# Four loads of v in one bunch, and an output projection one group later: a change to the order of work in a planned transformer kernel

## The chip, the cores and the metric

The kernel runs on one core of a Trainium2 chip. The metric is the device time of one execution in microseconds (us), from its start on the chip to its end; lower is better. The time of a version is the median of its runs.

The core has a matrix engine (TensorE, PE in the profile), a vector engine (VectorE, DVE), an engine for activations and copies (ScalarE, ACT), a general engine (GpSimd, POOL) and an engine that here does nothing but issue DMAs (SyncE, SP). Each works through its own list of instructions in order. ACT and POOL issue DMAs too, each from its own list. An instruction that waits for something holds up everything behind it on its engine.

## The reference

The input x has 2048 rows of 1024 bf16 numbers. The reference runs two kinds of layer, and the pair of them twice:

```python
x = A_x
x = x + _A_ref(_layernorm(x), A_wqkv, A_wo)
x = x + _B_ref(_layernorm(x), B_W_gate, B_W_up, B_W_down)
x = x + _A_ref(_layernorm(x), A_wqkv, A_wo)
x = x + _B_ref(_layernorm(x), B_W_gate, B_W_up, B_W_down)
```

`_A_ref` is attention over a dilated window. `x @ wqkv` (1024 x 3072) gives q, k and v with 32 heads of 32 numbers each. Row s looks at 8 rows only: s, s-2, ..., s-14 (rows before the first are masked). The 8 logits of a row and head are scaled, go through a softmax, weigh the same 8 rows of v, and the result is multiplied with `wo` (1024 x 1024).

`_B_ref` is a gated feed-forward layer: `gate = x @ W_gate` and `up = x @ W_up` (1024 x 3584 each), `h = relu(gate) * up`, and `h @ W_down` (3584 x 1024).

Both layers take the row-wise normalised x, (x - mean) / sqrt(var + eps), and add their result to x.

## The kernel before

**Tiling.** The rows are cut into 4 blocks of 512, and a block into 4 tiles of 128 rows. x stays in SBUF for the whole execution. All matrix products are groups of 8 (or 7) matmuls of 128 x 128 by 128 x 512 that add up in one PSUM accumulator; there are eight accumulators (`psum`, bufs=8). Weights come through a ring of five slabs (`ring`).

**Layers and blocks.** In the code layer 0 is the first attention, 1 the first feed-forward layer, 2 and 3 the second pair. TensorE first makes q, k and v of block 0 to block 3 of layer 0, one block after the other (`plan_proj`, L372). Then follow the feed-forward layer of block 0 (`plan_gu`, L728, then `plan_down`), and after it alternately pieces of attention and feed-forward work of the other blocks. The attention proper, between the projection and the multiplication with `wo`, has no matmul: DVE does it by products and additions.

**Block 0 of layer 0** has a way of its own to the logits, and the change lies there:

1. The matmuls of q and k give them feature-major. DVE multiplies and adds them over the features (`first_logits`, L473; `mul`, `add`) into two float32 buffers, `lacc0` and `lacc1`, with four of the eight window positions each.
2. Each half is stored to DRAM (`l_d<-lacc`, L528) and loaded back head-major (`lhm<-l_d`, L534), by two DMAs on SP. Both are planned in `turn(h)`, L525 to L542: the store 2.2 before the planned end of the half's last addition, the load 2.5 after it.
3. DVE folds the halves (`fold`), does the softmax (`soft_a`, `soft_b`; the exponential is ACT's), and then multiplies with v and adds, in 8 steps (`pv_mul` L629, `pv_add` L637 to L639). For this v must lie head-major in SBUF: `v_ready` (L664) plans four loads on SP, one for each tile of 128 rows (`vhm<-v_d`, L564). v itself was evicted by ACT from PSUM to `stage_v` and stored by a DMA that ACT issues.
4. The head outputs go to DRAM by a DMA of POOL (L640) and come back feature-major by four DMAs of SP (`load_o`, `oT<-o_d`, L648).
5. TensorE multiplies with `wo` (`plan_wo`, L701; matmuls L710, `acc_wo`), 2 groups for each of 4 tiles, and DVE adds each group to x (L717).

**Where step 5 stands.** TensorE does not wait idly for block 0's attention. It goes on with the projections of blocks 1 to 3. `wo_hook` (L819) names the group of block 3's projection behind which the eight groups of step 5 are put: `("q", 1, 1)`, the second of the four groups of the second half of q. `plan_proj` calls the hook behind that group (L466, L467), and the other groups of block 3 come after the eight.

**What follows.** With the addition of a tile of x, `plan_ln(1, 0)` (L212) begins the normalisation of block 0 for the feed-forward layer. For each tile: two sums on ACT (L238, L239). For each pair of tiles: four small DVE operations, the last giving `vpe` (L256 to L259), two small POOL operations `rstd` and `nb` (L260, L261), two normalisations on ACT (L267), and a transposing DMA on SP (`turn`, L273, `xnT<-xn_all`). The first gate group (L740, `acc_g`) of the feed-forward layer needs both transposes. The same function, with other times, normalises blocks 1 to 3 of layer 0 before their projections.

**What sets the order.** No scheduler reorders anything: the class `Plan` collects steps with planned times, and `run()` emits them sorted by time. TensorE's steps are laid end to end (`on_pe`, 0.216 for a matmul). DVE has a `chain`, the attention work, in its order, and `fixed` work with a due time (`on_dve`): before each link of the chain `_place_dve` first emits the fixed work that is due by then. The planned time at which a link ends sets the planned times of what hangs on it (`after`). DMAs have planned times only; their place among the other DMAs of the same engine comes from the sort. So a change to a planned time moves an instruction in the list of its engine. What it waits for at run time is then decided by the chip.

Completion of SP's and ACT's DMAs is counted on eight semaphores that are used in turn. In the programs' lists of waits each such DMA also waits for the one that used the same semaphore before it.

## Time and profile before

| | |
|---|---|
| time, median of 3 runs | 1617.26 us (1617.1 to 1617.5) |
| the profiled execution | 1618.13 us |
| its span, first to last instruction | 1616.4 us |
| granted TensorE clock, mean | 1.000 |
| share of the span in which the DMA engines work for SP's and ACT's queue (q1) | 66.9% |
| HBM read and written | 263.86 MB and 38.15 MB, 187 GB/s over the span |

In the profile a line such as `8.36 0.62 PE L404 MATMUL acc_v<-xnT,wqv 128*128 128x128 bf16 x8 [0.70 <-DMA wqv<-in_A_wqkv_dram]` reads: from 8.36 us after the start and for 0.62 us, TensorE ran 8 matmuls of line 404 that made `acc_v` out of `xnT` and `wqv`; before them it was idle for 0.70 us, and what ended the idle time was the landing of a DMA from `in_A_wqkv_dram` into `wqv`. SPq, ACTq and DVEq are the parts of an engine that issue DMAs or handle waits. A DMA has two times: the issue on the engine's queue, and the transfer up to its landing. Loads of a weight slab carry 1024 KB, a load of v 284 KB, a store of v 256 KB (section of DMA issues of the profile's page).

Where the first 200 us of the execution go, by TensorE's timeline: up to about 20 us the first pieces of v's projection for block 0, mixed with the transposes of the first tiles; then the rest of block 0's q, k and v up to 51.5 us; the projections of blocks 1 to 3, with the output projection of block 0 among the last, from 152.27 us; and from 190.26 us the feed-forward layer of block 0.

### The profile page before, as it was taken

Reading aid. Unit: us, or ns where it says so; the run is one execution under the profiler, and the core shown is the slowest. Engines: PE = TensorE matmul, PEld = TensorE weight load, DVE = VectorE, ACT = ScalarE, POOL = GpSimd, SP = SyncE. Lnnn points to the kernel's source line nnn. Section 1 sums busy time; section 2 is a strip of 40 time slices with the busy share of each in tenths; the row PEclk is TensorE's granted clock in tenths of the full one; section 3 lists DMA queues with packets and bytes.
Section 4 is the critical chain, followed back from the end, with each engine's and each line's share of the span. In section 5 each row is a group of like instructions: output and inputs, shape, how many; then the busy total and the mean of one; then the engine's idle time right before and its main releaser. Section 6 shows DMA issues by size and latency. Waiting matters only on the chain.

```text
span 1616.4 us, 19260 instructions
## 1 busy us (share of the span) xinstructions
PE 1610.0 (100%) x7656; PEld 745.6 (46%) x7656; DVE 1055.6 (65%) x1264; ACT 441.5 (27%) x703; POOL 126.2 (8%) x200
## 2 busy tenths in 40 slices
PE   9999999999999999999999999999999999999999
PEld 7444444444444444444444444444444444444444
DVE  6979999999999169860699517996998112211211
ACT  4642521305131241312413241133021311221110
POOL 2311000001011110011101110000000000000000
PEclk9999999999999999999999999999999999999999
DMA  8896797879966987669876699599856655574452
GB/s 256 227 242 154 203 215 201 209 177 214 220 182 204 243 187 210 197 212 232 194 204 195 209 226 219 165 274 225 224 163 194 178 169 163 176 188 151 157 167 68
DMA packets 444139, 319.02 MB, mean 197 GB/s; under 512 B 195696, under 2 KB 435728, under 8 KB 443792
## 3 DMA queue, kind: packets, MB, share of 16 engines
q1 hardware_dynamic: 414880, 285.59, 66.9%
q10 hardware_dynamic: 24368, 23.40, 4.8%
q0 software_dynamic: 4800, 8.80, 1.8%
q8 instruction: 60, 0.98, 0.3%
q14 instruction: 31, 0.25, 0.1%
HBM read 263.86 MB, written 38.15 MB: 187 GB/s over the span
## 4 chain that ended last, share of the span: by engine, by line
PE 93%; DVE 4%; DMA 2%; ACT 1%; issue 0%; SPq 0%; ACTq 0%; DVEq 0%
PE acc_u L740 24%; PE acc_g L740 24%; PE dacc L787 24%; PE acc_wo L710 7%; PE acc_v L404 5%; PE acc_k L404 5%; PE acc_q L404 4%; DVE pvt L629 1%; DVE lacc L522 1%; DVE pvt L637 1%; DMA l_d<-lacc 0%; DMA lhm<-l_d 0%; DVE prod L511 0%; DMA wqv<-in_A_wqkv_dram 0%; DVE pvt L638 0%; DMA oT<-o_d 0%
## 5 line engine op out<-in xcount | busy, mean ns | idle before, releaser
L740 PEld LDWEIGHTS <-ring 128*128 128x128 bf16 x3584 | 350.7, 98 | 422.9
L740 PE MATMUL acc_u<-xnT,ring 128*128 128x512 bf16 x1792 | 423.3, 379 | 0.0
L740 PE MATMUL acc_g<-xnT,ring 128*128 128x512 bf16 x1792 | 423.3, 379 | 0.0
L787 PE MATMUL dacc<-ring,hT 128*128 128x512 bf16 (+1 forms) x1820 | 388.1, 376 | 0.0
L755 DVE TENSOR_TENSOR hT<-acc_u,r 128x512 bf16<-128x512 f32 x224 | 154.2, 688 | 317.2 <-PE acc_u L740 312.1
L747 ACT ACTIVATE r<-acc_g 128x512 bf16<-128x512 f32 x224 | 133.5, 596 | 701.9 <-PE acc_g L740 690.4
L787 PEld LDWEIGHTS <-hT 128*128 128x128 bf16 x1820 | 178.1, 98 | 209.0
L404 PEld LDWEIGHTS <-ring 128*128 128x128 bf16 x1124 | 111.5, 100 | 124.0
L629 DVE TENSOR_TENSOR pvt<-a,vhm 128x4096 bf16<-128x4096 bf16 x64 | 146.2, 2284 | 0.1
L588 DVE TENSOR_TENSOR l<-l,pr 128x1024 f32<-128x1024 f32 x112 | 136.8, 1221 | 2.4
L578 DVE TENSOR_TENSOR pr<-qhm,khm 128x4096 bf16<-128x4096 bf16 x56 | 127.9, 2284 | 15.3 <-DMA khm<-k_d 15.3
L795 DVE TENSOR_TENSOR xb<-dacc,xb 128x512 bf16<-128x512 f32 (+1 forms) x49 | 32.8, 679 | 125.9 <-PE dacc L787 125.9
L404 PE MATMUL acc_k<-xnT,ring 128*128 128x512 bf16 x512 | 113.1, 379 | 0.0
L710 PE MATMUL acc_wo<-ring,oT 128*128 128x512 bf16 x512 | 111.8, 379 | 0.5 <-DMA oT<-o_d 0.5
L640 POOL DMA_DIRECT2D o_d<-ohm x64 | 35.2, 551 | 608.5 <-DVE ohm L639 594.6
L637 DVE TENSOR_TENSOR pvt<-pvt 128x2048 bf16<-128x2048 bf16 x64 | 78.1, 1221 | 1.3
L710 PEld LDWEIGHTS <-oT 128*128 128x128 bf16 x512 | 50.0, 98 | 61.2 <-DMA oT<-o_d 1.0
L404 PE MATMUL acc_v<-xnT,ring 128*128 128x512 bf16 (+1 forms) x356 | 76.1, 357 | 0.0
L260 POOL TENSOR_TENSOR rstd<-vpe,neg_half 128x2 f32<-128x2 f32 x30 | 32.0, 1066 | 552.5 <-DVE vpe L259 540.6
L414 ACT CAST stage_q<-acc_q 128x512 bf16<-128x512 f32 x56 | 32.2, 582 | 154.9 <-PE acc_q L404 150.6
L404 PEld LDWEIGHTS <-wqv 128*128 128x128 bf16 x556 | 52.0, 103 | 47.0 <-DMA wqv<-in_A_wqkv_dram 0.9
L588 DVE TENSOR_TENSOR l<-pr 128x1024 f32<-128x1024 bf16 x56 | 68.2, 1218 | 0.6
(88 smaller groups left out, 873.4 us busy)
## 6 DMA issues: line engine op xcount, KB each, us to landing
ring<-in_B_W_gate_dram SPq DMA_DIRECT2D x56, 1024.0 KB, 7.3
ring<-in_B_W_up_dram SPq DMA_DIRECT2D x56, 1024.0 KB, 5.6
ring<-in_B_W_down_dram SPq DMA_DIRECT2D x48, 1024.0 KB, 5.9
ring<-in_A_wqkv_dram SPq DMA_DIRECT2D x26, 1024.0 KB, 5.3
ring<-in_A_wo_dram SPq DMA_DIRECT2D x16, 1024.0 KB, 7.0
vhm<-v_d SPq DMA_DIRECT2D x32, 284.0 KB, 7.5
v_d<-stage_v ACTq DMA_DIRECT2D x32, 256.0 KB, 7.0
o_d<-ohm POOLq DMA_DIRECT2D x64, 128.0 KB, 3.7
```

Source lines behind the costliest of these rows:

```text
L404: nc.tensor.matmul(acc[:, t0 * P:t1 * P], lhsT=lhsT, rhs=xnT[(L, b)][:, t0:t1, kc, :], start=(kc == 0 and (nm, g, j) not in early), stop=( ...
L578: nc.vector.tensor_tensor(pr[:], st["q"][:], _ap(st["k"], HALO - DIL * w, [[HALO + P, DH], [1, P]]), op=ALU.mult)
L588: nc.vector.tensor_tensor(l[:], pr[:, 0:8] if i == 0 else l[:], pr[:, 8 * i + 8:8 * i + 16], op=ALU.add)
L629: nc.vector.tensor_tensor(tt[:], a_bc, v_sh, op=ALU.mult)
L637: nc.vector.tensor_tensor(tt[:, 0:4], tt[:, 0:4], tt[:, 4:8], op=ALU.add)
L640: nc.gpsimd.dma_start(_dram(o_d[b], g * DG * P, [[DH * P, P], [1, DG * P]]), o[:].rearrange("p d t -> p (d t)"))
L710: nc.tensor.matmul(acc[:], lhsT=st["oT"][:, c, t, :], rhs=ws[half]["t"][:, c, :], start=(c == 0), stop=(c == KC - 1))
L740: nc.tensor.matmul(acc[:], lhsT=w["t"][:, kc, (j % 4) * P:(j % 4 + 1) * P], rhs=xnT[(L, b)][:, :, kc, :], start=(kc == 0), stop=(kc == KC ...
L747: nc.scalar.activation(r[:], hold.pop(("g", j))[:], ACT.Relu)
L755: nc.vector.tensor_tensor(st["hT"][:, j, :], hold.pop(("u", j))[:], hold.pop(("r", j))[:], op=ALU.mult)
L787: nc.tensor.matmul(accs[(t, c0)][:], lhsT=st["hT"][:, j, t * P:(t + 1) * P], rhs=w["t"][:, jl, c0 - half * SLAB:c0 - half * SLAB + n], sta ...
L795: nc.vector.tensor_tensor(xt[:, c0:c0 + n], accs.pop((t, c0))[:], xt[:, c0:c0 + n], op=ALU.add)
```

## The change

Three edits, two of them in the plan of block 0's loads of v.

- In `v_ready` the four loads of v of block 0 had four planned times: the first two 0.8 apart, the last two just behind the planned time of the second load of logits (`tm["l_load"]`, which `turn(1)` wrote last). Now all four are planned 0.1 apart from the first's time on. The line that wrote `l_load` goes, since nothing reads it any more.
- In `wo_hook` the key `("q", 1, 1)` becomes `("q", 1, 2)`: the eight groups of block 0's output projection stand behind the third group of the second half of block 3's q.

In the lists of instructions this gives the following. On SP the third and fourth load of v stand directly behind the first two, ahead of the two transposes of block 2, the first store of logits and the first load of logits; before, they stood behind the second load of logits. On TensorE one group of `acc_q`, 8 matmuls, moves from behind the output projection to a place ahead of it. The planned times of what hangs on the projection move with it, so on DVE a product of a later block (L578) now stands ahead of the first additions of the output projection to x, and on ACT some evictions and issues of stores change places with the sums and normalisations of block 0. POOL's list is the same. No instruction is added or taken away.

```diff
@@ first_logits, turn(h)
                 plan.at(now - 2.2, store)
                 plan.at(now + 2.5, load)
                 tm[("l_in", h)] = now + 10.0
-                tm["l_load"] = now + 2.5
             return after
@@ plan_attn
         def v_ready():
             t = ends["v"] + 6.0
             if first:
-                return load((t, t + 0.8, tm["l_load"] + 0.1, tm["l_load"] + 0.2), (("v", v_d, ROW, HALO + P),))
+                return load(tuple(t + 0.1 * i for i in range(TPB)), (("v", v_d, ROW, HALO + P),))
@@ 
-    wo_hook = {("q", 1, 1): lambda: wo(0, 0)}
+    wo_hook = {("q", 1, 2): lambda: wo(0, 0)}
```

## The prediction

> **What bounds the kernel now.** I read the page first (totals, the chain that ended last), then the chain in order of time, then the timelines of PE, SP, DVE and ACT from 50 to 195 us, and the answers on single tiles for the time from a DMA's issue to its landing.

> ```profile
> span 1616.4 us, 19260 instructions
> ...
> PE 1610.0 (100%) x7656; PEld 745.6 (46%) x7656; DVE 1055.6 (65%) x1264; ACT 441.5 (27%) x703; POOL 126.2 (8%) x200
> ...
> PE 93%; DVE 4%; DMA 2%; ACT 1%; issue 0%; SPq 0%; ACTq 0%; DVEq 0%
> ```

> TensorE is busy for the whole span, at clock 1.00. A change elsewhere can therefore only add or remove a PE wait. The PE timeline has just one after the first 20 us, 0.47 us ahead of the first output projection:

> ```profile
> 152.27 13.99 PE L710 MATMUL acc_wo<-ring,oT 128*128 128x512 bf16 x64 [0.47 <-DMA oT<-o_d]
> ...
> 190.26 1.89 PE L740 MATMUL acc_g<-xnT,ring 128*128 128x512 bf16 x8
> ```

> The chain in order of time says what that wait stands on: block 0's attention, without a gap from the second half of its logits on.

> ```profile
> 80.22 2.30 DVE lacc L522
> 82.54 7.61 DMA l_d<-lacc
> 90.16 7.42 DMA lhm<-l_d
> 97.61 1.24 DVE lhm L549
> ...
> 145.07 2.29 DMA o_d<-ohm
> ...
> 147.63 4.59 DMA oT<-o_d
> ```

> Those two transfers sit in SP's queue behind what the change moves:

> ```profile
> 57.38 1.37 SPq L564 DMA_DIRECT2D vhm<-v_d  x2
> 65.14 6.08 SPq L273 DMA_TRANSPOSE xnT<-xn_all  x2
> 71.32 1.36 SPq L528 DMA_DIRECT2D l_d<-lacc  x1
> 78.67 0.34 SPq L534 DMA_DIRECT2D lhm<-l_d  x1
> 82.54 0.36 SPq L528 DMA_DIRECT2D l_d<-lacc  x1
> ```

> The second place with little slack is the first gate group at 190.26. It needs both transposes of the new normalised block 0; the second is issued at 181.81 and lands 6.2 us later, at 188.0. Its slack is 2.2 us.

> **The sum's base.** The profiled execution took 1618.13 us, 1.73 outside its span and 0.87 above the median of 1617.26. The sum is a difference in PE waits, and I add it to the median.

> **Part 1, the loads of v.** No work is added: four loads, all on SP, before and after. Two move from 90.5 to 58.8. Their issue (0.65 us each at 57.38) would lie in SP's pause from 58.75 to 65.14, where it waits for the normalisation of block 2. So much is free. But the program counts DMA landings on eight semaphores used in turn, and a DMA is issued only when the one before it on its semaphore has landed. With two more DMAs ahead, the lists of waits of the two programs give new partners:

> - The fourth load waits for a store of q that ACT issues at 61.85 and that lands 2.4 us later: 64.2.
> - Block 2's first transpose went at 65.14. It now waits for a store of k, issued at 65.62, landing after 3.4: 69.1, 3.9 later. The second follows 2.4 later at 71.5 and frees SP at 73.8. Both land by 79, and PE wants them at 92.9: covered by 14 us.
> - The first store of logits went at 71.32. It now waits for a store of q, issued 71.08, landing after 4.4: 75.5, so 4.2 late. It lands after 7.3, as before, at 82.8, and its load goes at 82.9.
> - The second store was ready when DVE ended at 82.52 and went at 82.54. SP now issues the first load just then, so it goes at 83.3: 0.8 late, with that load beside it.

> Its duration is the first unknown. Alone behind a nearly finished load it took 7.6. Weight loads of the same size that overlap took 10.4 and 10.9 (those issued at 184.0 and 186.7). The queues moved 317 GB/s from 82.5 to 90.2; load, store and two stores of v are 2.62 MB, 8.3 us at that rate, and about 1.5 us pass before a load's packets flow. I take 82.9 + 1.5 + 8.3 = 92.7, 2.5 late; the ends are 83.3 + 7.6 = 90.9 and 83.3 + 10.9 = 94.2. The second load took 7.4 with two loads of v behind it, the first one 6.1. I take its own 7.4, landing at 100.1, 2.5 late; the ends are 90.9 + 6.1 = 97.0 (0.6 early) and 94.2 + 7.4 = 101.6 (4.0 late).

> DVE waits for nothing but one exponential between 97.6 and 144.8, so all of this reaches the head outputs. ACT's exponential stands behind evictions that were themselves made later, 0.1 more. The shift is **2.6 us** (ends: 0.5 early, 4.1 late).

> The first load landing 4.2 us later also delays block 3's statistics on DVE and its normalisation on ACT, which holds up evictions: the one at 91.91 goes at 96.1. PE has eight accumulators of 1.73 us each, 13.8 us, so no wait. If that cover went, PE would stop near 101.

> **Part 2, the projection one group later.** One q group, 8 matmuls, 1.73 us, now runs before it. PE arrives at 152.27 - 0.47 + 1.73 = 153.5. The oT load lands at 152.2 + 2.6 = 154.8, and PE waits 1.3 where it waited 0.47: **+0.8**. With the loads as they were, this part alone would have removed the 0.47.

> **What is late next.** The same list of DVE instructions is planned anew. The adds of the projection's first tile stood before a product (L578, 2.28 us, 2.2 from start to start) and now stand after it. From 159.68 the add moves by 2.6 + 2.2. Row by row to the first pair's variance I get 0.3 more (one fold stands ahead of it now): 5.1 late. On ACT a DMA issue and an eviction of k now stand between the first pair's normalisation and the last tile's sums, and an eviction of v between the last two normalisations: 0.5, less 0.4 of waiting that goes, plus 0.7. So the second transpose is 5.9 late: 181.8 + 5.9 + 6.2 = 193.9. PE, 0.8 late, arrives at 191.1 and waits **2.8**.

> **Sum:** 0.8 + 2.8 = 3.6, with roundings 3.7 us: 1617.3 + 3.7 = **1621.0 us**. Nothing later is tight: the next groups waited for nothing before, and the weight loads behind the late transpose (184.0, 186.7) are wanted from 204.

> In that chain POOL's two small operations for the second pair are taken as before, 2.4 us. They took 1.59 and 0.69 there, 0.71 and 0.19 elsewhere; in both long cases they end right after the DVE operation beside them. Now short DVE operations stand beside them and then the 2.28 us product. Slipping in ahead of it saves 1.2; falling behind it costs 0.5.
> [...]

> **The rivals.**
> 1. *Not slower.* The two overlapping transfers take their low ends and POOL slips in. Then the shift is 0.5 early, PE finds oT landed, the second transpose is 2.8 - 1.2 = 1.6 late at 189.6, and PE comes at 189.8: 0.47 saved, 1616.8. It decides where the transpose is less than 1.8 late. For it: the 6.1 row, and two loads of v gone from 90.5. Against: DVE's new order alone costs 2.2.
> 2. *PE loses its clock in the wait.* The granted clock is 1.00 in every window, and no PE wait in this trace exceeds 1.5 us, so nothing here excludes that it falls in a longer one. If the first two groups after the wait ran at half speed, 2 x 1.73 us more: 1624.5. It decides if a wait of 2.8 us is long enough for that, of which the trace says nothing.
> [...]
> 3. *A small loss.* The semaphore partners land early, the shift is near 0.5, and the gate group waits about 1.5: net 1 us, 1618.3.
> 4. *The change gains.* PE can win back no more than 0.47 here, so faster by 0.2% is nearly excluded.

> **How the numbers follow.** What a measurement of this kernel can tell from no change is about 0.2%, 3.2 us: 1614.0 to 1620.5. The forecast case has 0.62 (its own range 1618.8 to 1622.8, about two thirds of it above 1620.5), the clock rival 0.13, the small loss 0.15, not slower 0.10. Slower: 0.41 + 0.13 = 0.54; within: 0.44; faster: 0.02. The range reaches from between the two small cases (1616.8 and 1618.3) to just past the clock rival, and leaves out the not-slower case and the tails: 1617.6 to 1624.6, about 0.83.

> **What would show it.** Right: first transpose of block 2 at about 69, logits stores at 75.5 and 83.3, second load landing near 100, PE waiting about 1.3 at L710 and 2.8 at L740. Wrong: if the two overlapped transfers land within 8 us, or the POOL pair takes under 1.3 us, the loss shrinks below 0.2%; if a clock under 1.00 follows PE's wait at L740, it is larger.

## The result, and the profile after

The changed kernel takes 1622.8 us (median of 8 runs, 1620.3 to 1624.1) against 1617.43 us of the kernel before, measured beside it: a ratio of 1.0028, with a 95% interval of 1.0017 to 1.0039. The forecast was 1621.0 us in a range of 1617.6 to 1624.6.

Its executions fall into two groups. Over all runs of the changed kernel in this study, nine took 1619.4 to 1621.5 us (median 1620.4) with a granted clock of 1.000, and ten took 1622.4 to 1624.1 us (median 1622.8) with 0.999 or 0.998. The profile is of the lower group: 1620.38 us beside a span of 1618.6. The page's totals:

```profile
span 1618.6 us, 19262 instructions
...
PE 1610.9 (100%) x7656; PEld 745.9 (46%) x7656; DVE 1055.8 (65%) x1264; ACT 441.4 (27%) x703; POOL 125.4 (8%) x200
```

The work is the same; the span is 2.2 us longer. TensorE's timeline shows where (start, busy time, and in brackets the idle time before and what ended it). Lines of the changed kernel's code from 541 on have numbers one lower than before:

```profile
154.05 13.99 PE L709 MATMUL acc_wo<-ring,oT 128*128 128x512 bf16 x64 [0.28 <-DMA oT<-o_d]
...
192.49 1.89 PE L739 MATMUL acc_g<-xnT,ring 128*128 128x512 bf16 x8 [2.01 <-DMA xnT<-xn_all]
```

The wait at the output projection went from 0.47 to 0.28 us, and a new one of 2.01 us stands at the first gate group. 0.24 us more had been lost before 121 us.

SP's timeline shows what became of the loads of logits:

```profile
57.18 9.14 SPq L563 DMA_DIRECT2D vhm<-v_d  x4
68.65 6.89 SPq L273 DMA_TRANSPOSE xnT<-xn_all  x2
76.14 0.69 SPq L528 DMA_DIRECT2D l_d<-lacc  x1
82.93 0.34 SPq L534 DMA_DIRECT2D lhm<-l_d  x1
83.36 0.39 SPq L528 DMA_DIRECT2D l_d<-lacc  x1
93.71 0.33 SPq L534 DMA_DIRECT2D lhm<-l_d  x1
```

The four loads of v occupy SP's queue for 9.14 us where two took 1.37, since the fourth goes only at 65.78, when a store of q on its semaphore has landed (65.77). Block 2's transposes go 3.5 us late, the first store of logits 4.8, its load 4.3, and the second load 3.6. The first transpose goes at 68.65, behind a store of k that landed at 68.57. The chain in order of time says what the first store of logits waited for last; it is a DMA with which it shares no data, a store of q that ACT had issued:

```profile
71.23 4.85 DMA q_d<-stage_q
...
76.14 6.77 DMA l_d<-lacc
```

This wait is not the whole delay. The two transposes themselves keep SP's queue until 75.54 (68.65 and 6.89 us), and the store of q adds 0.5 us to that.

The late first load also reaches the softmax. The statistics of block 3 stand behind it on DVE, and block 3's normalisations (L267) stand ahead of the exponential (L610) on ACT:

```profile
99.75 1.24 ACT L267 ACTIVATE xn_all<-xb,nb,rstd 128x1024 bf16<-128x1024 bf16 x1 [0.75 <-POOL nb L261]
...
101.90 1.24 ACT L267 ACTIVATE xn_all<-xb,nb,rstd 128x1024 bf16<-128x1024 bf16 x1 [0.45 <-ACT stage_v L414]
...
104.54 1.06 ACT L610 ACTIVATE L<-L 128x1024 f32<-128x1024 f32 x1 [0.44 <-ACT stage_q L414]
```

On POOL's timeline the second pair of small operations, which took 1.59 and 0.69 us before, has become short:

```profile
181.32 1.06 POOL L260 TENSOR_TENSOR rstd<-vpe,neg_half 128x2 f32<-128x2 f32 x1 [6.92 <-DVE vpe L259]
182.47 0.21 POOL L261 TENSOR_TENSOR nb<-neg,rstd 128x2 f32<-128x2 f32 x1
```

### The profile page after: what moved, and what is told of

Same layout as the page of the kernel before. It is cut to its first block, busy times and chain, and to the rows that moved or that the text cites. A ratio compares the mean times of both kernels' runs of the same rounds, so it can differ in the third digit from the quotient of the medians.

```text
span 1618.6 us, 19262 instructions
## 1 busy us (share of the span) xinstructions
PE 1610.9 (100%) x7656; PEld 745.9 (46%) x7656; DVE 1055.8 (65%) x1264; ACT 441.4 (27%) x703; POOL 125.4 (8%) x200
## 4 chain that ended last, share of the span: by engine, by line
PE 91%; DVE 4%; DMA 2%; issue 1%; ACT 1%; POOL 0%; ACTq 0%; SPq 0%; DVEq 0%; POOLq 0%
PE acc_g L739 24%; PE acc_u L739 24%; PE dacc L786 24%; PE acc_wo L709 6%; PE acc_q L404 5%; PE acc_k L404 5%; PE acc_v L404 4%; DVE pvt L628 1%; DMA xnT<-xn_all 1%; DVE l L587 1%; DVE pvt L636 1%; DMA l_d<-lacc 0%; DVE pr L577 0%; DMA lhm<-l_d 0%; DMA wqv<-in_A_wqkv_dram 0%
```

## The experiments

The theory after this result: the moved loads shift the semaphore partners and make the head outputs 1.5 to 2 us late; the later projection hides that at the output projection, but DVE's new order makes the second transpose of block 0 late, and TensorE waits at the first gate group; a wait of about 2 us costs TensorE its clock in some executions. Each part has a rival below. The medians, by the place of the loads of v and by the projection:

| loads of v \ projection | where it was | one group later | one group later, additions as before |
|---|---|---|---|
| as before | 1617.4 to 1617.7 (kernel before) | 1617.99 | 1617.17 |
| all four ahead of block 2's transposes | 1622.57 | 1622.8 and 1622.36 (changed kernel) | 1618.16 |
| two behind the first store of logits | 1617.45 | | 1617.62 |

### The loads of v alone

```diff
 (changed kernel)
-    wo_hook = {("q", 1, 2): lambda: wo(0, 0)}
+    wo_hook = {("q", 1, 1): lambda: wo(0, 0)}
```

> The changed kernel with the projection back behind the second group of q, so only the loads of v are moved. Theory (the gate group's wait comes mainly from the new place of the additions on DVE; the loads of v cost about 1.6 us on the way to the head outputs): TensorE arrives at the output projection near 152.0 us, oT lands as in the changed kernel near 154.0, so TensorE waits about 2.0 us there and none at the first gate group (second transpose landing near 190.4, TensorE there near 192.0). Time about 1.5 us above the kernel before, 1618.9. Rival (the late loads of logits alone carry the loss): the gate group still waits 2 us behind the other wait, time 1621 or more. Second rival (any wait of about 2 us can cost TensorE its clock): some executions 2 to 3 us above 1618.9, with a granted clock of 0.998 or 0.999.

Measured: 1622.57 us (1621.6 to 1623.8, 6 runs), ratio 1.0031 (1.0020 to 1.0043), and a clock of 0.998 or 0.999 in all six. So this part alone loses as much as the whole change (1622.36 us in the same set of runs), 3.7 us more than the theory's 1618.9. TensorE's timeline has all of the wait at the output projection and none at the gate group:

```profile
155.21 0.61 PE L709 MATMUL acc_wo<-ring,oT 128*128 128x512 bf16 x1 [3.39 <-DMA oT<-o_d]
156.03 15.93 PE L709 MATMUL acc_wo<-ring,oT 128*128 128x512 bf16 x61 [0.22 <-issue]
```

The stretches of the span around it (length, PE, PEld, DVE, ACT, POOL, granted clock, DMA share, GB/s) show the second rival at work:

```profile
154.00:156.00 2.00, 0.61 (x1) 0.28 (x3) 1.93 (x3) 0.00 (x0) 0.00 (x0) 0.51 1.18 303
...
160.00:161.00 1.00, 1.00 (x4) 0.33 (x3) 0.96 (x2) 0.00 (x0) 0.00 (x0) 0.57 1.44 156
161.00:162.00 1.00, 1.00 (x6) 0.49 (x5) 0.93 (x3) 0.00 (x0) 0.00 (x0) 1.00 1.46 154
```

From the end of the wait to about 160.9 the clock is 0.50, 5.7 us that do the work of 2.8. The wait was 1.4 us longer than expected: the last head outputs came 0.6 us later than in the profile of the changed kernel, and their store took 4.14 us, 0.6 more than there and 1.9 more than in the kernel before. Why the store takes so long is open; in the other profiles with the loads of v ahead it took 2.3 to 3.5 us.

### The projection alone

```diff
 (kernel before)
-    wo_hook = {("q", 1, 1): lambda: wo(0, 0)}
+    wo_hook = {("q", 1, 2): lambda: wo(0, 0)}
```

> The kernel before with only the projection moved behind the third group of q. Theory: oT lands at 152.2 us as in the kernel before, TensorE comes at 153.5 and waits for nothing there (0.47 us won); the additions stand behind a product of 2.28 us on DVE, so the second transpose of block 0 lands 2 to 3 us later, 190.1 to 191, and TensorE, there at 189.8, waits 0.3 to 1.2 us. Time within 0.7 us of the kernel before. Rival (the loads of v alone make the loss): no wait at all, 0.47 us faster. Clock 1.000 in every execution, since the wait is short.

Measured: 1617.99 us (11 runs), ratio 1.0003 (0.9994 to 1.0012), clock 1.000 throughout. As expected, 0.47 us are won at one place and nearly given back at the other:

```profile
190.15 1.89 PE L740 MATMUL acc_g<-xnT,ring 128*128 128x512 bf16 x8 [0.37 <-DMA xnT<-xn_all]
```

### The whole change, with the additions where they were

```diff
 (changed kernel, plan_wo)
-                plan.on_dve(e + T_EV, 0.7, add(half, t), ...)
+                plan.on_dve(e + T_EV - 8 * MM * ((L, b) == (0, 0)), 0.7, add(half, t), ...)
```

> The changed kernel, but the additions of block 0's output projection are given due times 1.73 us earlier, so that on DVE, ACT, SP and POOL they and all that hangs on them stand where they stood before; the loads of v and TensorE's order are those of the changed kernel. Theory: oT as in the changed kernel, a wait of about 0.3 us at the output projection; the second transpose lands 2.2 us or more sooner than in the changed kernel, near 190.2, TensorE comes at 190.2 to 190.5, and the gate group waits at most 0.3 us. Time 1617.3 (1617.0 to 1617.8), clock 1.000 in all executions. Rival (the late loads of logits carry the loss): a wait of 1.5 us or more stays, 1619 or more.

Measured: 1618.16 us (11 runs), ratio 1.0003 (0.9994 to 1.0012), 0.4 us above the range that was expected: most of the loss is gone (the changed kernel took 1622.36 us beside it), though the loads of v are still all ahead. Ten executions took 1617.9 to 1619.0 at clock 1.000, one 1621.83 at 0.999. It was this one that was profiled; there oT came late enough for a wait of 2.62 us at the output projection (and none at the gate group), and the clock fell behind it:

```profile
156.08 15.67 PE L709 MATMUL acc_wo<-ring,oT 128*128 128x512 bf16 x62 [2.62 <-DMA oT<-o_d]
```

```profile
156.00:157.00 1.00, 0.87 (x3) 0.41 (x5) 0.96 (x3) 0.00 (x0) 0.00 (x0) 0.76 1.33 254
157.00:158.00 1.00, 1.00 (x4) 0.39 (x3) 1.00 (x1) 0.00 (x0) 0.00 (x0) 0.50 1.39 218
...
160.00:161.00 1.00, 1.00 (x6) 0.43 (x5) 1.00 (x1) 0.00 (x0) 0.00 (x0) 1.00 1.45 148
```

So the order on DVE is what turns the late loads into the wait at the gate group. The expected wait of 0.3 us at the projection holds for most executions at best: in the profiled one the first store of logits went at 77.57 instead of 76.14 and the head outputs were stored 2.3 us later than in the profile of the changed kernel, with the same order on SP up to there.

### The changed kernel again

> The changed kernel, unchanged. Theory (its executions fall into two groups, 1620.3 to 1620.9 at clock 1.000 and 1622.7 to 1624.1 at 0.998 or 0.999, because TensorE loses its clock for one or two windows after the wait of about 2 us at the first gate group): the same two groups again, the gap between them 2 to 3 us; if the profiled execution is of the upper group, its granted clock falls below 1.00 only between 190 and 200 us. Rival (a cause elsewhere in the execution): the clock falls at another place, or the upper group is longer without it.

> The changed kernel again, for a profile of an execution of its upper group (ten of 17 so far). Theory: the wait at the first gate group is 2.0 to 3 us as in the two profiles of the lower group, and the clock falls to 0.50 for 3.0 to 3.4 us within the first two groups behind it and nowhere else; the execution is then 1.5 to 1.7 us longer than its waits alone make it. Rival (the upper group is another, longer wait): no clock below 1.00, but a wait of 4 us or more.

> As the run before it, a further profile of the changed kernel: in the lower group (about 1620.6) no clock below 1.00 and waits that add up to 2 to 3 us, in the upper group (about 1622.9) a fall to 0.50 behind the first gate group. Rival as there.

Measured: nine runs with a median of 1622.36 us, in the same two groups (five of nine with a clock below 1.000), and two further executions of 1620.19 and 1620.17. All three profiles were of the lower group, so no profile shows the clock's fall in the changed kernel itself; that it lies behind the gate group's wait is inferred from the other kernels. The kernel before isn't free of it either: one of its 26 executions beside these took 1620.19 us at a clock of 0.999. The waits at the gate group that did not cost the clock were 2.79, 2.02 and 2.14 us. The first of them:

```profile
154.02 13.99 PE L709 MATMUL acc_wo<-ring,oT 128*128 128x512 bf16 x62 [0.38 <-DMA oT<-o_d]
193.24 1.89 PE L739 MATMUL acc_g<-xnT,ring 128*128 128x512 bf16 x8 [2.79 <-DMA xnT<-xn_all]
```

A wait of 2.79 us without a loss here, and one of 2.62 with a loss in the experiment above: the length alone doesn't decide.

### When a wait costs the clock

```diff
 (kernel before)
     with tc.manual_schedule():
         plan.run()
+        probe()
```

```python
def probe():
    fill = at_pool.tile([P, DH * P], BF16, tag="pr", name="fill", bufs=2)
    ...
    for r in range(6):
        for i in range(13):
            acc = psum.tile([P, BLK], F32, tag="acc", name="acc_probe")
            n = 37 + 2 * ((5 * i + 3 * r) % 4)
            for m in range(n):
                nc.tensor.matmul(acc[:], lhsT=pl[:], rhs=_ap(ident, 0, [[0, TPB], [1, P]]), start=(m == 0), stop=(m == n - 1))
            nc.vector.tensor_copy(mark[:], acc[:, 0:8])
            for c in (min(i, 7), i - 7):
                if c > 0:
                    f = fill[:, 0:512 * c]
                    nc.vector.tensor_tensor(f, f, f, op=ALU.max)
            nc.vector.tensor_copy(pl[:], zeros[:])
```

> The kernel before, followed by a probe: 78 times 37 to 43 matmuls of 128x512 (8 to 9.3 us) and then a wait for a chain on DVE whose length goes from about 0.7 us to 4.5 us in 13 steps of 0.3 us, six times over. The time is not compared, since the probe is added work. Theory (TensorE loses its clock when the idle time that falls into one window of about 3.4 us passes some share of it; the window does not start with the wait): below about 2 us never, above about 3.4 us always, and between them sometimes, depending on where the wait begins; the loss is a stretch of 3.4 us, or twice that, at half clock. Rival (a fixed length decides): one length below which the clock never falls and above which it always does. Second rival (only a full idle window counts): no fall for any wait under 3.4 us.

Measured, from TensorE's timeline, a stretch at half clock being one in which the starts of the matmuls lie 0.43 instead of 0.216 us apart:

| TensorE's wait, us | waits | followed by a stretch at half clock |
|---|---|---|
| 0.36, 0.70, 0.96, 1.23, 1.50, 1.76 | 36 | 0 |
| 2.03 | 6 | 3 |
| 2.30 | 6 | 1 |
| 2.76 | 6 | 5 |
| 3.02, 3.29, 3.56 | 18 | 18 |
| 3.82 | 5 | 5 |

By the trace's record of the granted clock each of these stretches is 3.41 us long, but for one of 6.83. A stretch can begin before the wait ends, so the matmuls behind it take 1.3 to 1.7 us longer than usual (2.8 us behind the one of 6.83). Two waits of the same length, the first followed by 43 matmuls that take 11.14 us instead of 9.5, the second by 41 that take the usual 9.02:

```profile
1687.69 11.14 PE L910 MATMUL acc_probe<-ident,pl 128*128 128x512 bf16 x43 [2.03 <-DVE pl L916]
```

```profile
1839.19 9.02 PE L910 MATMUL acc_probe<-ident,pl 128*128 128x512 bf16 x41 [2.03 <-DVE pl L916]
```

Both rivals fall. The same wait has both outcomes, so no fixed length decides, and waits far below 3.4 us suffice.

The windows of the theory can be seen in the same record. Over the 900 us of the probe every change of the clock lies on one grid of 3.413 us, to within 0.01 us, and neither a wait nor a fall shifts the grid. Laid over the waits, the grid cuts some of them in two. In all 32 waits with a fall at least 2.03 us of one window were idle, and the clock fell at the end of that window; in the 45 without a fall no window held more than 2.01 us. The waits of the other kernels agree:

| wait that ends at, us | length | its parts in successive windows | half clock |
|---|---|---|---|
| 2012.78 (probe) | 2.76 | 2.76 | yes |
| 2315.34 (probe) | 2.75 | 1.04, 1.72 | no |
| 2302.74 (probe) | 2.30 | 2.30 | yes |
| 1850.51 (probe) | 2.30 | 1.20, 1.10 | no |
| 156.08 (additions as before) | 2.62 | 2.62 | yes |
| 155.21 (loads of v alone) | 3.39 | 2.21, 1.18 | yes |
| 193.24 (changed kernel again) | 2.79 | 1.22, 1.57 | no |
| 192.49 (changed kernel) | 2.01 | 0.65, 1.36 | no |

So here about 2 us of idleness within one window decide, and it is the position of the wait on the grid that looks like chance. The ends of matmuls are modelled in a trace, so the bound is good to some hundredths of a us at best.

### The loads of v ahead, but counted elsewhere

```diff
 (changed kernel with the projection where it was; the load of one tile)
-                    nc.sync.dma_start(st[nm][32 * tq:32 * tq + 32, :, :],
+                    eng = nc.gpsimd if (L, b, nm) == (0, 0, "v") and tq > 1 else nc.sync
+                    eng.dma_start(st[nm][32 * tq:32 * tq + 32, :, :],
```

> Only the loads of v are moved (projection where it was, as in the run that took 1622.6 us), but the third and fourth are issued by POOL. POOL's DMAs are counted on other semaphores, so the transposes of block 2, the stores of logits and their loads keep the partners that they had in the kernel before, though the loads of v go as early as in the changed kernel. Theory (the loss of the moved loads is the shift of the semaphore partners: the first store of logits waits for a store of q that is issued at 71.1): the first store of logits goes at 71.3 again, the second load of logits lands at 97.6 or a little before, TensorE waits at most 0.6 us for oT, clock 1.000; time 1617.5 (1617.0 to 1618.2). Rival (the two loads themselves, as traffic or as POOL's work, do the harm): the store of logits goes on time but the loads of logits still land 1 us or more late, TensorE waits 1.5 us or more; time 1619 or more.

Measured: 1619.78 us (1617.3 to 1622.8, 11 runs), ratio 1.0013 (1.0004 to 1.0021), three of eleven with a clock below 1.000. That lies between theory and rival. POOL's timeline and then SP's, of its fastest execution (1617.31 us), show part of the reason:

```profile
60.33 1.63 POOL L564 DMA_DIRECT2D vhm<-v_d  x2
```

```profile
64.80 8.32 SPq L273 DMA_TRANSPOSE xnT<-xn_all  x2
73.23 0.54 SPq L528 DMA_DIRECT2D l_d<-lacc  x1
```

The transposes of block 2 go at 64.80, as early as in the kernel before (65.14): no partner holds them here. But with the two moved loads still under way (they land at 66.3 and 69.0) the first transpose takes 8.0 us to land instead of 6.1, the two keep SP for 8.32 us instead of 6.08, and the first store of logits goes at 73.23, neither at 71.3 nor at 76. So in this execution loads this far ahead make the store 1.9 us late without any shift of its partners, and the theory is not the whole cause. TensorE has no wait here; where the slower executions lose their time is not shown.

In the profile of the changed kernel and the six others with all four loads ahead on SP, the first transpose goes within 0.1 us of the landing of the store of k (68.3 to 69.3). The second leaves the queue within 0.9 us of the first one's landing, as it does in all thirteen profiles without the probe; why is not shown. So the second, which now follows sooner behind the first, takes 2.9 to 5.1 us of the queue where it took 2.25 before. The first store of logits then goes behind whichever is later, the queue or the store of q. They are at most 1.0 us apart, and in two of the seven (the loads of v alone, and the changed kernel again) it was the queue.

### The loads of v behind the first store of logits

```diff
 (kernel before)
-                return load((t, t + 0.8, tm["l_load"] + 0.1, tm["l_load"] + 0.2), (("v", v_d, ROW, HALO + P),))
+                return load((t, t + 0.8, 57.6, 57.7), (("v", v_d, ROW, HALO + P),))
```

> The kernel before with the third and fourth load of v moved to a place directly behind the first store of logits on SP, 18 us earlier than in the kernel before and 13 us later than in the changed kernel. From the programs' lists of waits: the transposes of block 2, the first store of logits, and the second store keep partners that have long landed; the first load of logits has a store of q as partner that lands at 78.65, where its store of logits lands at 78.6. Theory (what the moved loads cost is the stores of q and k that block 2's transposes and the first store of logits wait for when the loads are put ahead of them): the first store of logits goes at 71.3 as before, its load at 78.7, the second load of logits lands near 97.6, TensorE waits 0.5 us for oT as before; time that of the kernel before within 0.5 us, where the run with all four loads ahead took 5.0 us more. Rival (two loads of v ahead of the loads of logits cost by their traffic, wherever they stand): the store of logits takes 1.5 us more beside them, TensorE waits 2 us or more, with clock losses; time 1620 or more.

Measured: 1617.45 us (11 runs), ratio 0.9999 (0.9990 to 1.0008), clock 1.000 throughout, and no wait of TensorE after the first 24 us of the profiled execution. SP's timeline:

```profile
65.19 6.19 SPq L273 DMA_TRANSPOSE xnT<-xn_all  x2
71.47 1.30 SPq L528 DMA_DIRECT2D l_d<-lacc  x1
72.83 3.53 SPq L564 DMA_DIRECT2D vhm<-v_d  x2
79.45 0.35 SPq L534 DMA_DIRECT2D lhm<-l_d  x1
82.58 0.37 SPq L528 DMA_DIRECT2D l_d<-lacc  x1
91.04 0.33 SPq L534 DMA_DIRECT2D lhm<-l_d  x1
```

The two loads go 18 us earlier than in the kernel before and cost nothing in sum. The transfers of logits do change: the first load takes 7.6 us instead of 6.1 beside the loads of v and lands 2.3 us later, and the second, with no loads of v behind it any more, takes 4.8 instead of 7.4 and lands 1.7 us earlier (at 95.9, where 97.6 was expected). In sum the head outputs are stored 0.7 us earlier (144.41 after 145.07). So the rival's price is there, on another transfer than it named, but it isn't paid at the end, and the rival as stated, that the traffic costs time wherever the loads stand, falls. What costs is their place ahead of the transposes and the first store of logits.

The gain at the second load is seen throughout. It took 7.2 to 7.5 us in the three profiles in which two loads of v stand behind it, and 4.6 to 5.3 in the ten in which they don't.

### POOL beside a long product

```diff
 (changed kernel, plan_ln)
-                    plan.on_dve(clock[0], 0.7, lambda: small_a(t // 2), ...)
+                    plan.on_dve(clock[0] + 1.0 * ((L, b, t) == (1, 0, TPB - 1)), 0.7, lambda: small_a(t // 2), ...)
```

> The changed kernel, but the small DVE operations of block 0's second pair come one fold (1.45 us) later, so that POOL's two operations for it stand beside the product of 2.28 us and no longer beside short operations. [...] Rival (POOL's times are its own): the pair takes 1.3 us, the wait is 3.5 us, time 1624 to 1626.

Measured: 1628.43 us (4 runs), ratio 1.0062 (1.0047 to 1.0077), clock 0.997 or 0.998 in all. POOL's rows, the product beside them on DVE, and TensorE's wait:

```profile
183.96 2.66 POOL L260 TENSOR_TENSOR rstd<-vpe,neg_half 128x2 f32<-128x2 f32 x1 [8.43 <-DVE vpe L259]
186.70 0.69 POOL L261 TENSOR_TENSOR nb<-neg,rstd 128x2 f32<-128x2 f32 x1
```

```profile
183.79 2.28 DVE L577 TENSOR_TENSOR pr<-qhm,khm 128x4096 bf16<-128x4096 bf16 x1
```

```profile
198.24 3.57 PE L739 MATMUL acc_g<-xnT,ring 128*128 128x512 bf16 x8 [7.88 <-DMA xnT<-xn_all]
```

The product began 0.17 us ahead of POOL's first operation, which ended 0.55 us after the product and took 2.66 us instead of 1.06; the pair took 3.43 instead of 1.36. So POOL's times are not its own, and the rival falls. In the trace of the kernel before, too, POOL's first operation ends 0.55 us after a DVE operation with both inputs in SBUF that began ahead of it (at 178.61 after L588 at 178.06, at 593.61 after L578 at 593.06), and takes 0.71 us beside an addition with one input in PSUM (L717, at 168.65). That DVE in turn waits for POOL is not shown: an L588 that begins during that operation of 0.71 us, at 169.07, takes its usual 1.22. TensorE's wait of 7.88 us is longer than the rival's 3.5, and the time 2.4 us above its range: against the second profile of the changed kernel (2.79 us) 1.45 came from the later place, 2.1 from POOL, 0.7 from a transpose that took 7.3 instead of 6.6 us, and 0.5 from a DMA issue that now stood, with an eviction, between the last two normalisations on ACT; the remaining 0.3 is the balance of smaller differences. The first gate groups then ran at half clock, 3.57 us for 8 matmuls.

### Without the costs

Two kernels that keep the additions' order: the kernel before with the later projection, and the same with the loads of v behind the first store of logits.

```diff
 (kernel before)
-    wo_hook = {("q", 1, 1): lambda: wo(0, 0)}
+    wo_hook = {("q", 1, 2): lambda: wo(0, 0)}
-                plan.on_dve(e + T_EV, 0.7, add(half, t), ...)
+                plan.on_dve(e + T_EV - 8 * MM * ((L, b) == (0, 0)), 0.7, add(half, t), ...)
```

> The kernel before with the projection behind the third group of q and the additions given due times 1.73 us earlier, so that DVE, ACT, SP and POOL keep their order. Theory: nothing is late, both waits of TensorE are gone (0.47 at the output projection; the first gate group has 1.8 us of slack): 0.5 us faster than the kernel before, 1617.0, clock 1.000 in all executions, no execution above 1618.5. Rival (the order on DVE is not what made the first gate group late): a wait of 0.4 us or more there, as in the run with the projection alone moved, 1617.5 to 1618.

> The same place of the loads of v, and also the projection behind the third group of q with the additions planned as before. Theory: both waits of TensorE go, 1617.1, no execution above 1618.5, like the run with the later projection and the loads of v where they were. Rival (traffic of the early loads): 1618 or more.

Measured: 1617.17 us (1616.9 to 1617.8, 11 runs; ratio 0.9994, 0.9985 to 1.0003) and 1617.62 us (1617.0 to 1618.3; ratio 1.0000, 0.9991 to 1.0009). Neither can be told from the kernel before by its median. Neither profile has a wait of TensorE left after the first 24 us, as the theory said; the second median is still 0.5 us above its theory's 1617.1.

## Why the prediction came out as it did

The direction, the two places and the mechanism were right, and the time lay in the range; 1.8 us are missing between 1621.0 and the median. Against the lower group, which keeps its clock, the forecast is 0.6 us too high. That the median is a clear loss is in part luck: the waits alone, which are the forecast's own case, give 1620.4, just inside the 1614.0 to 1620.5 that it counted as no change. The fall of the clock, a rival there, takes it past that.

- **The partners.** Forecast: first transpose of block 2 at 69.1, stores of logits at 75.5 and 83.3, first load at 82.9. Measured: 68.65, 76.14, 83.36 and 82.93. The times are right, and the partners of the transposes too. But the forecast had the transposes free SP at 73.8, and they did at 75.54; it took 2.4 us for the second, which kept the queue for 5.04. The store of q, which was to hold the first store for 1.7 us beyond that, held it for 0.5. That the store's time came out is partly luck.
- **The overlapped transfers.** The second store was to take 9.4 us and its load 7.4, landing at 100.1. They took 10.35 and 4.7, landing at 98.4. The load's price was the mis-sized one: it took less than either row (6.1 and 7.4) that bounded it. "I take its own 7.4" took over a row with two loads of v behind it, and the change takes just these away.
- **The exponential.** That it "stands behind evictions that were themselves made later, 0.1 more" was ten times too small: DVE waited 2.18 us for it instead of 1.12. Block 3's normalisations and some evictions stand in front of it in both kernels, and the late first load made them late enough to hold it up. With the opposite error of the load, the head outputs came 1.9 us late, not 2.6.
- **The output projection.** Forecast: a wait of 1.3 us. Measured: 0.28 and 0.38 in two profiles and 0.1 or less in two more, since the head outputs were less late than forecast and the load of oT took 3.25 us where it had taken 4.59 (the store ahead of it took 1.2 more). The term of +0.8 was in truth -0.2. It is the term that varies most: the same loads gave a wait of 2.62 us in the profile with the additions as before.
- **DVE's new order.** First variance 5.1 us late by forecast; vpe came 4.8 late (173.17 after 168.40). Right, and shown by giving the additions their old places: the wait at the gate group goes, and 4.2 us with it (1622.36 and 1618.16).
- **POOL's pair.** Taken as before, 2.4 us, by the row; it took 1.36, in all five profiles with this order on DVE. With 1.36 in the row's place the sum is 2.7 us, an estimate; the lower group lies 3.0 above the kernel before. The row was not POOL's own: the operation of 1.59 us ended 0.55 us after an addition of 1.22 us on DVE (L588, up to 178.06), the one of 1.06 ends 0.55 us after an addition of 0.69 us (L594, up to 181.84), and the experiment with the product beside POOL has the same 0.55 us.
- **The gate group.** Forecast 2.8, measured 2.01 to 2.79 in four profiles.
- **The clock.** This was a rival with 0.13, and it came in ten of nineteen executions. The term that was mis-sized is "If the first two groups after the wait ran at half speed, 2 x 1.73 us more", with its small chance. The half speed was an assumption there; the traces show it, 0.50 (the loads of v alone, the probe). But the fall is cheaper, 1.3 to 1.7 us for one window in the probe, and far more frequent, because a wait of 2 to 2.8 us is just where the grid decides. The two groups of times lie 2.4 us apart, more than one such fall; whether the waits of the upper group are also longer, no profile shows.
- **Not slower, small loss.** Neither came. The small loss needed head outputs about 0.5 us late, and not slower needed them early; they were 1.9 us late.

## What to carry to other kernels

When DMAs are moved in a queue, list for every DMA behind them which earlier one it must see landed, across all engines that share the semaphores: free time in the queue says nothing about that, and a place a few steps further on can be free. Look also at how long the DMAs behind them then take, on the queue and to land: here one load gained 2.6 us from the move. When an operation is moved by planned time, look at what the planner does to the other engines: here the move that hid one delay made another. And where TensorE bounds a kernel, price a wait at more than its length if it is as long as those that cost the clock here (3 of the probe's 6 waits of 2.03 us, all 23 of 3.02 or more): one stretch at half clock added 1.3 to 1.7 us.
